# The gate vector's turn as a full product in the PSUM pair of the second turn, and K's first pieces reordered with shorter fillers

## The chip, the cores and the metric

The kernel runs on one core of one Trainium2 chip. The time is the device time of one execution in microseconds (us).

Names used below: PE is the matmul engine, PEld its weight load, ACT, DVE and POOL are ScalarE, VectorE and GpSimd, SP is the engine whose queue (SPq) issues most DMAs. "Landing" is the time at which the last of a DMA's semaphore increments stands in the trace. Times within an execution are counted from the start of the profiled span.

## The reference, cut to what matters

```
g = sigmoid((x * gate_w).sum(-1, keepdims=True))
a = linear_attention(x, wqkv, wo)     # q, k, v = x @ wqkv; phi(k), phi(q); ...
b = mixer_mlp(x, w1, w2, w3, w4)
return g * a + (1 - g) * b            # x: 1 x 2048 x 640, bf16
```

The first work of the kernel is K, the product of x with the K columns of `wqkv`, for 16 chunks of 128 rows each. The gate's logit is one more column of that product: `gate_w`, turned into a column, is put into column 640 of K's weights.

## The kernel before

PE needs x transposed. The first chunk is turned on PE (five 128x128 transposes); the other 15 come through transposing DMAs. `gate_w` arrives as 5 rows of 128 and is turned on PE into 128x5. Fillers (`warmup`: products of ones into a PSUM pair that nobody reads) keep PE busy while data arrives; they are meant to make its clock rise early.

```
    load_x(0, 1)                                   # SP queue
    aq.dma_start(g5[:], ...)                       # ACT queue: gate_w, 5 x 128
    load_wk(sp, 1); load_wk(aq, 0); load_wk(aq, 2); load_wk(sp, 3); load_wk(aq, 4)
    for c0, c1 in ((1, 2), (2, 3), (3, 4), (4, 6), (6, 8), (8, 12), (12, 16)):
        load_xT(c0, c1)                            # transposing DMAs on SP's queue
    ...
    warmup(6)                                      # six 512-wide fillers
    warmup(3, P)                                   # three 128-wide
    kp = pair()
    turns = [(pair()[:, 0, :].bitcast(BF16), a, b) for a, b in ((0, 2), (2, DC))]
    tg = warm[:, 0, :].bitcast(BF16)               # the fillers' own pair
    for n, (ptb, a, b) in enumerate(turns):
        for dc in range(a, b):
            nc.tensor.transpose(ptb[...], x_sb[:, 0, dc * P:(dc + 1) * P], ident[:])
        nc.vector.tensor_copy(xT[:, a:b, 0:P], ...)
        if n == 0:
            nc.tensor.transpose(tg[:, 0:DC], g5[:], ident[0:DC, 0:DC])
            nc.vector.tensor_copy(wk_sb[:, :, D], tg[:, 0:DC])
    warmup(3, P)
    for dc in range(DC):
        k_mm(kp, 0, (dc,))                         # one piece: two products, 320 and 321 wide
        if dc < DC - 1:
            warmup(1, 2 * P)
    k_evac(kp, 0)
    for c in range(1, NCH):                        # chunks 1 to 15, no fillers
        pt = pair()
        k_mm(pt, c, range(DC))
        k_evac(pt, c)
```

Of the kernel before, what the change touches and what calls it, by code (L numbers as in the profile page):

```python
# [9 lines left out]
BF16 = mybir.dt.bfloat16  # L10
# [6 lines left out]
def kernel(  # L17
# [13 lines left out]
    nc = tc.nc  # L31
    P = 128
    S, D = A_x.shape[1], A_x.shape[2]
# [6 lines left out]
    DC = D // P  # L40
    HD = D // 2
# [19 lines left out]
    const = ctx.enter_context(tc.tile_pool(name="const", bufs=1))  # L61
# [7 lines left out]
    def pair():  # L69
        return ps.tile([P, 2, 512], F32, name="pp")  # L70
# [14 lines left out]
    r_bf = const.tile([P, TS], BF16)  # L85
    ident = const.tile([P, P], BF16)
    g5 = const.tile([DC, P], BF16)
    mhalf = const.tile([P, CPT], F32)
    hmask = const.tile([P, H], F32)
    zbd = const.tile([P, DC, H], BF16)  # L90
# [16 lines left out]
    wk_sb = st1.tile([P, DC, D + 16], BF16)  # L107
# [73 lines left out]
    def phi(dst, src, n):  # L181
        e = e_p.tile([P, 1024], BF16, name="e")
        ev = e[:, 0:n]
        if len(src.shape) == 3:
            ev = ev.rearrange("p (h e) -> p h e", h=src.shape[1])
        nc.scalar.activation(ev, src, ACT.Exp)  # L186
        nc.vector.tensor_scalar(e[:, 0:n], e[:, 0:n], 1.0, 1e-6, op0=ALU.min, op1=ALU.add)
        nc.vector.scalar_tensor_tensor(dst, src, 0.0, ev, op0=ALU.max, op1=ALU.add)  # L188

    def k_mm(pt, c, dcs, hfs=(0, 1), last=DC - 1):  # L190
        for dc in dcs:
            for hf in hfs:
                n = HD + hf
                nc.tensor.matmul(pt[:, hf, 0:n], lhsT=xT[:, dc, c * P:(c + 1) * P],  # L194
                                 rhs=wk_sb[:, dc, hf * HD:hf * HD + n], start=(dc == 0), stop=(dc == last))

    def k_evac(pt, c):
        nc.scalar.copy(ylog[:, c:c + 1], pt[:, 1, HD:HD + 1])
        phi(pk[:, c, :].rearrange("p (h e) -> p h e", h=2), pt[:, :, 0:HD], D)

    warm = pair()
    one = nc.const_aps.tensor(1.0, (P, TS), BF16)

    def warmup(n, w=TS):
        for i in range(n):
            nc.tensor.matmul(warm[:, 1, 0:w], lhsT=one[:, 0:P], rhs=one[:, 0:w], start=True, stop=True)  # L206

    warmup(6)
    warmup(3, P)
    kp = pair()  # L210
    turns = [(pair()[:, 0, :].bitcast(BF16), a, b) for a, b in ((0, 2), (2, DC))]
    tg = warm[:, 0, :].bitcast(BF16)
    for n, (ptb, a, b) in enumerate(turns):
        for dc in range(a, b):
            nc.tensor.transpose(ptb[:, (dc - a) * P:(dc - a + 1) * P], x_sb[:, 0, dc * P:(dc + 1) * P], ident[:])
        nc.vector.tensor_copy(xT[:, a:b, 0:P], ptb[:, 0:(b - a) * P].rearrange("p (c s) -> p c s", c=b - a))
        if n == 0:
            nc.tensor.transpose(tg[:, 0:DC], g5[:], ident[0:DC, 0:DC])
            nc.vector.tensor_copy(wk_sb[:, :, D], tg[:, 0:DC])
    warmup(3, P)  # L220
    for dc in range(DC):
        k_mm(kp, 0, (dc,))
        if dc < DC - 1:
            warmup(1, 2 * P)
    k_evac(kp, 0)
    for c in range(1, NCH):
        pt = pair()
        k_mm(pt, c, range(DC))
        k_evac(pt, c)
# [375 lines left out]
```

## Time and profile before

| | before |
|---|---|
| median of 3 runs | 265.8 us (265.54 to 266.0) |
| span of the profiled execution | 264.0 us |
| PE busy | 99% of the span |
| chain of waits that ended last | 97% PE |
| start of K chunk 0, of chunk 1, of chunk 8 | 4.82, 7.12, 16.66 us |

The first lines are the page's busy times and its chain by engine (shares of the span), of the kernel before.

```profile
PE 260.3 (99%) x1744; PEld 161.8 (61%) x1744; DVE 139.5 (53%) x271; ACT 85.1 (32%) x126; POOL 21.9 (8%) x67
...
PE 97%; ACT 1%; DVE 0%; issue 0%
```

PE sets the time from front to end. Busy PE is not useful PE, though: the fillers count as busy too. The next lines are the timeline of PE at the front (start us, duration us, engine, source line, operation, shapes, count). Durations include each product's pipeline, so the rate is read from one start to the next.

```profile
0.83 3.04 PE L206 MATMUL pp<-const-bfloat16-1.0 128*128 128x512 bf16 x9 [0.83 <-PEq L589]
3.66 0.42 PE L215 MATMUL pp<-ident,x_sb 128*128 128x128 bf16 x2
4.01 0.18 PE L218 MATMUL pp<-ident,g 5*128 5x5 bf16 x1
4.13 0.50 PE L215 MATMUL pp<-ident,x_sb 128*128 128x128 bf16 x3
4.55 0.48 PE L206 MATMUL pp<-const-bfloat16-1.0 128*128 128x128 bf16 x3
4.82 0.74 PE L194 MATMUL pp<-wk_sb,xT 128*128 128x320 bf16 x2
5.36 0.42 PE L206 MATMUL pp<-const-bfloat16-1.0 128*128 128x256 bf16 x1
5.57 0.57 PE L194 MATMUL pp<-wk_sb,xT 128*128 128x320 bf16 x2
5.97 0.27 PE L206 MATMUL pp<-const-bfloat16-1.0 128*128 128x256 bf16 x1
6.08 0.44 PE L194 MATMUL pp<-wk_sb,xT 128*128 128x320 bf16 x2
6.36 0.27 PE L206 MATMUL pp<-const-bfloat16-1.0 128*128 128x256 bf16 x1
6.46 0.44 PE L194 MATMUL pp<-wk_sb,xT 128*128 128x320 bf16 x2
6.74 0.27 PE L206 MATMUL pp<-const-bfloat16-1.0 128*128 128x256 bf16 x1
6.85 0.57 PE L194 MATMUL pp<-wk_sb,xT 128*128 128x320 bf16 x3
```

(The window ends at 7.2 us; the third product of the last line is the first of chunk 1, at 7.12.) Two things are to be seen. First, a piece of K and its filler take 0.75 us from 4.82 to 5.57, and 0.38 us from 6.08 to 6.46, where the next piece starts: the clock doubles in between. The packed trace's clock record begins at 5.83 us, at full speed, and that is called the rise. The mean clock that the page and each run list leaves the time before it out: it reads 1.0 here in spite of the slow start. Second, the 5-row gate turn (the 5*128 line) leaves holes: the transpose before it starts at 3.77 and the next after it at 4.13, for one product that has five columns; and the 128-wide filler behind the last transpose (4.32) starts only at 4.55, since it writes the PSUM pair that DVE must first empty (its copy ended at 4.50).

### The profile page before, as it was taken

What the parts mean: (1) busy time and instruction counts of PE and PEld (TensorE: products, weight loads), DVE (VectorE), ACT (ScalarE), POOL (GpSimd) and SP (SyncE); (2) the same over time, 40 slices, a digit from 0 to 9 for tenths busy, and PEclk for the clock granted to TensorE, in tenths of its full rate; (3) what the DMA queues carried; (4) which work ended last, traced back from release to release, by engine and by line L of the source; (5) the groups of instructions that cost most, each with busy time, mean ns of one, the idle gap of its engine ahead of it and who ended that gap; (6) DMA issues with size and microseconds to landing.
All of it is one profiled execution on the core that took longest, in us unless ns stands there. A gap on an engine that the chain in (4) does not pass through costs nothing.

```text
span 264.0 us, 4272 instructions
## 1 busy us (share of the span) xinstructions
PE 260.3 (99%) x1744; PEld 161.8 (61%) x1744; DVE 139.5 (53%) x271; ACT 85.1 (32%) x126; POOL 21.9 (8%) x67
## 2 busy tenths in 40 slices
PE   8999999999999999999999999999999999999995
PEld 4777555788754654556667555667565576555743
DVE  1688778899948597964503455413356223112132
ACT  1555554321165725612502221412131332142100
POOL 7100120012210040001000001000001000000000
PEclk9999999999999999999999999999999999999999
DMA  7999987016673726700132000051100051100011
GB/s 200 179 208 370 375 252 298 0 29 123 124 101 75 79 51 161 239 0 2 25 75 77 25 0 2 0 99 52 50 0 2 0 101 52 50 0 2 0 50 50
DMA packets 46285, 23.62 MB, mean 89 GB/s; under 512 B 35770, under 2 KB 45626, under 8 KB 46266
## 3 DMA queue, kind: packets, MB, share of 16 engines
q1 hardware_dynamic: 45824, 22.86, 34.1%
q10 hardware_dynamic: 442, 0.49, 0.5%
q8 instruction: 13, 0.21, 0.4%
q14 instruction: 6, 0.05, 0.1%
HBM read 12.21 MB, written 2.62 MB: 56 GB/s over the span
## 4 chain that ended last, share of the span: by engine, by line
PE 97%; ACT 1%; DVE 0%; issue 0%
PE pp L484 21%; PE pp L464 21%; PE pp L194 8%; PE pp L311 8%; PE pp L417 8%; PE pp L448 8%; PE pp L345 8%; PE pp L236 8%; PE pp L206 2%; PE pp L472 1%; PE pp L493 1%; ACT m_sb L385 1%; PE pp L364 1%; PE pp L251 0%; DVE oc L512 0%; PE pp L383 0%
## 5 line engine op out<-in xcount | busy, mean ns | idle before, releaser
L464 PE MATMUL pp<-lnxT,w_sb 128*128 128x512 bf16 x260 | 60.4, 379 | 0.0
L484 PE MATMUL pp<-w_sb,h 128*128 128x256 bf16 (+3 forms) x416 | 58.0, 299 | 0.1
L466 ACT ACTIVATE h<-pp 128x1024 bf16<-128x1024 f32 (+1 forms) x28 | 26.9, 962 | 82.2 <-PE pp L464 82.2
L484 PEld LDWEIGHTS <-h 128*128 128x128 bf16 x416 | 39.3, 98 | 18.0 <-issue 1.3
L464 PEld LDWEIGHTS <-w_sb 128*128 128x128 bf16 x260 | 25.5, 98 | 26.8
L500 DVE SCALAR_TENSOR_TENSOR oc<-pp,omg,x 128x640 bf16<-128x640 f32 x14 | 12.0, 881 | 41.4 <-ACT h2x L475 21.3
L451 DVE SCALAR_TENSOR_TENSOR x<-pp,gate,x 128x640 f32<-128x640 f32 x16 | 13.9, 868 | 29.4 <-PE pp L448 29.4
L420 DVE TENSOR_TENSOR x<-pp,x_sb 128x640 f32<-128x640 f32 x16 | 13.1, 820 | 22.6 <-PE pp L417 22.6
L186 ACT ACTIVATE e<-pp 128x640 bf16<-128x640 f32 (+1 forms) x26 | 21.5, 827 | 9.6 <-PE pp L236 9.6
L448 PE MATMUL pp<-m_sb,pqT 128*128 128x320 bf16 x160 | 24.3, 299 | 0.0
L417 PE MATMUL pp<-w_sb,hsT 128*128 128x320 bf16 x160 | 23.9, 299 | 0.1
L194 PE MATMUL pp<-wk_sb,xT 128*128 128x320 bf16 (+1 forms) x160 | 22.9, 302 | 0.0
L311 PE MATMUL pp<-x_sb,pk 128*128 128x320 bf16 (+1 forms) x160 | 22.3, 300 | 0.0
L236 PE MATMUL pp<-xT,hsT 128*128 128x512 bf16 x100 | 21.7, 379 | 0.0
L311 PEld LDWEIGHTS <-pk 128*128 128x128 bf16 x160 | 18.8, 117 | 3.5
L417 PEld LDWEIGHTS <-hsT 128*128 128x128 bf16 x160 | 15.6, 98 | 8.2 <-issue 0.2
L448 PEld LDWEIGHTS <-pqT 128*128 128x128 bf16 x160 | 15.7, 98 | 7.7
L194 PEld LDWEIGHTS <-xT 128*128 128x128 bf16 x160 | 15.8, 99 | 6.1
L345 PE MATMUL pp<-lnxT,w_sb 128*128 128x512 bf16 x80 | 17.9, 379 | 0.0
L236 PEld LDWEIGHTS <-hsT 128*128 128x128 bf16 x100 | 11.8, 118 | 9.7
L281 POOL TENSOR_SCALAR rstd<-mv 128x4 f32<-128x4 f32 (+1 forms) x11 | 3.4, 314 | 156.5 <-DVE mv L287 156.5
L188 DVE SCALAR_TENSOR_TENSOR pk<-pp,e 128x640 bf16<-128x640 f32 x16 | 13.2, 825 | 1.7
(77 smaller groups left out, 194.9 us busy)
## 6 DMA issues: line engine op xcount, KB each, us to landing
out_dram<-oc SPq DMA_DIRECT2D x14, 160.0 KB, 1.8
w_sb<-in_B_w_dram SPq DMA_DIRECT2D x1, 2080.0 KB, 10.0
w_sb<-in_B_w_dram SPq DMA_DIRECT2D x1, 1296.0 KB, 8.4
x_sb<-in_A_x_dram SPq DMA_DIRECT2D x2, 640.0 KB, 10.4
x_sb<-in_A_x_dram SPq DMA_DIRECT2D x1, 1120.0 KB, 7.9
wo_sb<-in_A_wo_dram SPq DMA_DIRECT2D x6, 160.0 KB, 6.0
w_sb<-in_B_w_dram SPq DMA_DIRECT2D x1, 864.0 KB, 5.7
hsT<-in_A_wqkv_dram SPq DMA_DIRECT2D x1, 800.0 KB, 5.3
```

Of the source, the lines that this page charges most:

```text
L186: nc.scalar.activation(ev, src, ACT.Exp)
L188: nc.vector.scalar_tensor_tensor(dst, src, 0.0, ev, op0=ALU.max, op1=ALU.add)
L194: nc.tensor.matmul(pt[:, hf, 0:n], lhsT=xT[:, dc, c * P:(c + 1) * P], rhs=wk_sb[:, dc, hf * HD:hf * HD + n], start=(dc == 0), stop=(dc == ...
L236: nc.tensor.matmul(pt[:, t % 2, :], lhsT=wq_sb[:, dc, :].rearrange("p (m j) -> p j m", j=DC)[:, j], rhs=xT[:, dc, t * TS:(t + 1) * TS], st ...
L311: nc.tensor.matmul(pt[:, hf, 0:HD + hf], lhsT=w, rhs=x_sb[:, c, hf * HD:(hf + 1) * HD + hf], start=(c == 0), stop=(c == NCH - 1))
L345: nc.tensor.matmul(pt[:, i, :], lhsT=w, rhs=lnxT[t][:, dc, :], start=(dc == 0), stop=(dc == DC - 1))
L417: nc.tensor.matmul(pt[:, hf, 0:HD], lhsT=hsT[:, fc, 2 + c * P:2 + (c + 1) * P], rhs=w2_sb[:, fc, hf * HD:(hf + 1) * HD], start=(fc == 0), ...
L448: nc.tensor.matmul(pt[:, hf, 0:HD], lhsT=pqT[:, j, c * P:(c + 1) * P], rhs=m_sb[:, j, hf * HD:(hf + 1) * HD], start=(j == 0), stop=(j == D ...
L451: nc.vector.scalar_tensor_tensor(x1, pt[:, :, 0:HD], gate[:, c:c + 1], x1, op0=ALU.mult, op1=ALU.add)
L464: nc.tensor.matmul(pt[:, k, :], lhsT=w3_sb[:, dc, fc * P:(fc + 1) * P], rhs=lnT[:, dc, :], start=(dc == 0), stop=(dc == DC - 1))
L466: nc.scalar.activation(h2[:, 2 * i * TS:(2 * i + n) * TS], pt[:].rearrange("p h e -> p (h e)")[:, 0:n * TS], ACT.Gelu_apprx_tanh)
L484: nc.tensor.matmul(dst, lhsT=st[t]["h2"][:, fc * TS + cc * P:fc * TS + (cc + 1) * P], rhs=w4_sb[:, fc, a:b], start=start and fc == 0, stop ...
```

## The change

The intent: close both holes (a full 128-row product in the pair of the second turn instead of a 5-row one in the fillers' pair), start earlier with fewer fillers, and take K's pieces in the order in which their weights land.

```diff
+    g5z = const.tile([P, P], BF16)
...
+    nc.vector.memset(g5z[:], 0.0)
+    nc.vector.tensor_copy(g5z[0:DC, :], g5[:])
-    warmup(6)
+    warmup(5)
     warmup(3, P)
...
-        if n == 0:
-            nc.tensor.transpose(tg[:, 0:DC], g5[:], ident[0:DC, 0:DC])
-            nc.vector.tensor_copy(wk_sb[:, :, D], tg[:, 0:DC])
+        if b == DC:
+            nc.tensor.matmul(pt[:, 1, 0:DC], lhsT=g5z[:], rhs=ident[:, 0:DC], start=True, stop=True)
...                                                # after the copy of the second turn:
+        if b == DC:
+            nc.vector.tensor_copy(wk_sb[:, :, D], pt[:, 1, 0:DC])
-    warmup(3, P)
-    for dc in range(DC):
-        k_mm(kp, 0, (dc,))
-        if dc < DC - 1:
-            warmup(1, 2 * P)
+    warmup(4, P)
+    for n, dc in enumerate((1, 0, 3, 2, 4)):
+        if n > 1:
+            warmup(1, P)
+        k_mm(kp, 0, (dc,), first=1, last=4)
+    warmup(2, P)
```

(`k_mm` now takes the first piece as an argument; the order stands inline here.)

More of the change, by code (lines that the diff above doesn't have):

```diff
@@ L188, in phi, with k_mm @@
         nc.vector.scalar_tensor_tensor(dst, src, 0.0, ev, op0=ALU.max, op1=ALU.add)
-    def k_mm(pt, c, dcs, hfs=(0, 1), last=DC - 1):
+    def k_mm(pt, c, dcs, first=0, last=DC - 1):
         for dc in dcs:
-            for hf in hfs:
+            for hf in range(2):
                 n = HD + hf
                 nc.tensor.matmul(pt[:, hf, 0:n], lhsT=xT[:, dc, c * P:(c + 1) * P],
-                                 rhs=wk_sb[:, dc, hf * HD:hf * HD + n], start=(dc == 0), stop=(dc == last))
+                                 rhs=wk_sb[:, dc, hf * HD:hf * HD + n], start=(dc == first), stop=(dc == last))
     def k_evac(pt, c):
@@ L199, in k_evac @@
         phi(pk[:, c, :].rearrange("p (h e) -> p h e", h=2), pt[:, :, 0:HD], D)
+    k0_order = (1, 0, 3, 2, 4)
     warm = pair()
@@ L206, in warmup @@
             nc.tensor.matmul(warm[:, 1, 0:w], lhsT=one[:, 0:P], rhs=one[:, 0:w], start=True, stop=True)
-    warmup(6)
+    nc.vector.memset(g5z[:], 0.0)
+    nc.vector.tensor_copy(g5z[0:DC, :], g5[:])
+    warmup(5)
     warmup(3, P)
     kp = pair()
-    turns = [(pair()[:, 0, :].bitcast(BF16), a, b) for a, b in ((0, 2), (2, DC))]
-    tg = warm[:, 0, :].bitcast(BF16)
-    for n, (ptb, a, b) in enumerate(turns):
+    turns = [(pair(), a, b) for a, b in ((0, 2), (2, DC))]
+    for pt, a, b in turns:
+        ptb = pt[:, 0, :].bitcast(BF16)
         for dc in range(a, b):
             nc.tensor.transpose(ptb[:, (dc - a) * P:(dc - a + 1) * P], x_sb[:, 0, dc * P:(dc + 1) * P], ident[:])
+        if b == DC:
+            nc.tensor.matmul(pt[:, 1, 0:DC], lhsT=g5z[:], rhs=ident[:, 0:DC], start=True, stop=True)
         nc.vector.tensor_copy(xT[:, a:b, 0:P], ptb[:, 0:(b - a) * P].rearrange("p (c s) -> p c s", c=b - a))
-        if n == 0:
-            nc.tensor.transpose(tg[:, 0:DC], g5[:], ident[0:DC, 0:DC])
-            nc.vector.tensor_copy(wk_sb[:, :, D], tg[:, 0:DC])
-    warmup(3, P)
-    for dc in range(DC):
-        k_mm(kp, 0, (dc,))
-        if dc < DC - 1:
-            warmup(1, 2 * P)
+        if b == DC:
+            nc.vector.tensor_copy(wk_sb[:, :, D], pt[:, 1, 0:DC])
+    warmup(4, P)
+    for n, dc in enumerate(k0_order):
+        if n > 1:
+            warmup(1, P)
+        k_mm(kp, 0, (dc,), first=k0_order[0], last=k0_order[-1])
+    warmup(2, P)
     k_evac(kp, 0)
```

## The prediction

> **What bounds the kernel now.** PE: 99% of a 264.0 us span on the page, 97% of the chain of waits. The listing of waits for PE gives only the start (0.8 us). So a shift at the front reaches the end unless something else steps in. The change touches only the first 7 us, before the second K chunk.
>
> **The front, from PE's timeline, start to start.** At first a 512-wide filler takes 0.427 us, a 128-wide one 0.107, a 320-wide K product 0.267. From 5.84 us on they take half (0.136 and, 256 wide, 0.109). This is the clock gate of the Trainium skill, "TensorE: Matmul & The Clock Gate", Part 1; its two rates agree with this trace. Transposes start at 3.67, the first K piece at 4.83, the second K chunk at 7.12. Two holes are the gate vector's: about 0.14 us around its 5-row turn (3.77 to 4.21), and 0.13 us where the filler waits for VectorE to empty the PSUM pair that turn shared with the fillers (4.32 to 4.61).
>
> **What the change does.**
> - One 512-wide filler less: transposes start 0.43 us earlier (3.24), just after the x chunk lands (3.09).
> - Gate turn as a full 128-row product in another pair: both holes go, about 0.27 us. Its memset and copy run on an idle VectorE before 3 us.
> - Fillers before K: four 128-wide for three, +0.11 us. PE is ready at about 4.30, but the first weight piece lands at 4.50 (piece 1, now first; piece 0, before first, at 4.76). K starts at about 4.55, 0.28 us earlier; PE idles 0.25 us instead.
> - Fillers between the pieces: 0.54 us become three 128-wide plus two behind, about 0.33 us. Part of that is lost if the clock still rises at 5.84. The second chunk then starts at about 6.83 instead of 7.12: 0.3 us gained. Its x landed at 6.60, so nothing holds it.
>
> **How much reaches the end.** Little. The K chunks read x through transposing DMAs, whose issue does not depend on PE. The one for chunks 8 to 11 is issued at 9.41 and takes 7.0 us to land: 16.44. Before, PE loads chunk 8's first weights at 16.53, only 0.09 us later. Moved 0.3 us forward, PE would want them at 16.23 and must wait; its product can start at about 16.60 instead of 16.66. All other landings have at least 0.38 us of slack. So of 0.3 us at 7 us I expect 0.06 us behind chunk 8, the rest as a new wait of PE there. The landing can jitter, so up to 0.3 us may survive in some runs.
>
> **Prediction: 265.7 us, range 265.3 to 266.2.** Faster by over 2%: 0.01; within 2%: 0.98; slower by over 2%: 0.01.
>
> **What the profile would show.**
> - Transposes from 3.24 us, no hole at the gate turn.
> - PE idle about 0.25 us ahead of K's first product, until the weights' DMA; K at 4.55.
> - Second chunk at 6.8 to 6.9.
> - A PE wait on the transposing DMA at chunk 8 near 16.5 us, and all starts behind it within 0.1 us of before. If chunk 8 starts at 16.37, the DMA landed earlier and the gain is 0.3 us.
>
> **What would make it wrong.** The clock gate: if the hole before K, or the 5-wide product's low activity, makes the clock rise later, each K product until then costs 0.13 us more; a whole window of 3.4 us (that page's figure) at half rate would lose up to 1.7 us (estimate). If it rises earlier, 0.2 us more are gained at the front and lost again at chunk 8. A late x chunk (0.05 to 0.15 us of margin) would move everything.

## The result

The changed kernel took 265.97 us (median of 4 runs, 265.76 to 266.23), the kernel before 265.7 us in its 4 runs. The ratio is 1.0009, 95% interval 0.9992 to 1.0027: the same. A ratio is the mean time of one kernel's runs over that of the other's of the same rounds, so it is not quite the ratio of the medians quoted. With the two repeats below the changed kernel has 16 runs of mean 265.93 us.

First the chain by engine on the page of the changed kernel, to be read against the 97% PE of before.

```profile
PE 91%; SPq 3%; DMA 3%; ACT 1%; DVE 0%; issue 0%
```

Then its PE timeline at the front.

```profile
0.83 2.61 PE L208 MATMUL pp<-const-bfloat16-1.0 128*128 128x512 bf16 x8 [0.83 <-PEq L595]
3.24 0.74 PE L219 MATMUL pp<-ident,x_sb 128*128 128x128 bf16 x5
3.77 0.21 PE L221 MATMUL pp<-ident,g5z 128*128 128x5 bf16 x1
3.84 0.59 PE L208 MATMUL pp<-const-bfloat16-1.0 128*128 128x128 bf16 x4
4.22 0.89 PE L195 MATMUL pp<-wk_sb,xT 128*128 128x320 bf16 x4
4.95 0.22 PE L208 MATMUL pp<-const-bfloat16-1.0 128*128 128x128 bf16 x1
5.56 0.43 PE L195 MATMUL pp<-wk_sb,xT 128*128 128x320 bf16 x2 [0.40 <-DMA wk_sb<-in_A_wqkv_dram]
...
6.49 0.28 PE L208 MATMUL pp<-const-bfloat16-1.0 128*128 128x128 bf16 x2
6.75 2.49 PE L195 MATMUL pp<-wk_sb,xT 128*128 128x320 bf16 x17
```

The front did what it was meant to do: transposes from 3.24, a gate product that costs 0.07 us to the next start, K at 4.22, chunk 1 at 6.75 instead of 7.12, 0.37 us earlier. PE now waits for weights inside the first chunk (0.40 us before piece 3).

Then the changed kernel's chain of waits from 9 to 40 us (start us, us, what), and its PE timeline around chunk 8.

```profile
8.14 1.71 SPq L122
9.85 0.04 issue
9.89 7.03 DMA xT<-in_A_x_dram
16.92 0.05 issue
16.97 11.07 PE pp L195 x80
```

```profile
14.78 1.80 PE L195 MATMUL pp<-wk_sb,xT 128*128 128x320 bf16 x12
16.97 2.22 PE L195 MATMUL pp<-wk_sb,xT 128*128 128x320 bf16 x15 [0.39 <-DMA xT<-in_A_x_dram]
```

The chain now runs over the transposing DMA of chunks 8 to 11. It was issued at 9.89 and landed at 16.92, and chunk 8 started at 16.97, where the kernel before had started it at 16.66 without a wait (its landing: 16.43). The kernel before shows one run of products there:

```profile
14.75 4.52 PE L194 MATMUL pp<-wk_sb,xT 128*128 128x320 bf16 x32
```

So at chunk 1 PE was 0.37 us ahead of the kernel before, and at chunk 8 it was 0.31 us behind it: 0.68 us were lost between the two. Of these 0.11 went at chunk 4, whose x landed at 10.91, and 0.55 at chunk 8. From there on both executions run alike: the last product of the kernel starts 244.44 us after chunk 8 in the one, 244.45 in the other.

That one trace leaves a question. Was the DMA late because of the change, or by scatter, and would the front's gain show if chunk 8 did not hold it?

### The profile page after: what moved, and what is told of

It reads as the page before. It is cut to its first block, busy times and chain, and to the rows that moved or that the text cites. A ratio compares the mean times of both kernels' runs of the same rounds, so it can differ in the third digit from the quotient of the medians.

```text
span 264.3 us, 4277 instructions
## 1 busy us (share of the span) xinstructions
PE 259.8 (98%) x1745; PEld 161.4 (61%) x1745; DVE 139.8 (53%) x273; ACT 85.1 (32%) x126; POOL 21.8 (8%) x67
## 4 chain that ended last, share of the span: by engine, by line
PE 91%; SPq 3%; DMA 3%; ACT 1%; DVE 0%; issue 0%
PE pp L490 21%; PE pp L470 21%; PE pp L317 8%; PE pp L423 8%; PE pp L454 8%; PE pp L351 8%; PE pp L242 8%; PE pp L195 4%; SPq L122 3%; DMA xT<-in_A_x_dram 3%; PE pp L478 1%; PE pp L499 1%; ACT m_sb L391 1%; PE pp L370 1%; PE pp L257 0%; DVE oc L518 0%
## 5 line engine op out<-in xcount | busy, mean ns | idle before, releaser
L188 DVE TENSOR_SCALAR e<-e 128x640 bf16<-128x640 bf16 (+1 forms) x26 | 9.5, 365 | 9.4 <-ACT e L187 8.1
```

## The experiments

Theory 1: PE is held at chunk 8 by a landing that does not depend on PE; the front's gain is given back there. Theory 2: the change itself makes the DMA chain late. Theory 3: its lateness is scatter between executions. A further rival: the front's gain in the trace was the luck of an early clock rise (4.33 us here, 5.83 before), not the change's.

The twelve runs came in three sets of four: a1, b1, c1, d1 on one chip; then a2, c2, e1, e2, and last b2, c3, g1, o1, both on another chip. The first set shares 11 executions of the kernel before, of mean 265.88 us. The other two share 12 (those of the second set and one more), of mean 266.18 us.

### a1, a2: the changed kernel again

No edit.

> The changed kernel once more, to see what of its one trace repeats. Theory 1 (PE is held at K chunk 8 by the transposing DMA of chunks 8 to 11, so the front's gain is given back there): chunk 8 starts within 0.1 us of that landing, 16.4 to 17.0 us, and the ratio to before is 0.999 to 1.002. Theory 2 (the change itself slows the SyncE queue's DMA chain by 0.4 us): that chain is late again, the second transposing DMA is again issued in 1.78 us, and landing is again 16.9. Theory 3 (the chain's lateness is scatter between executions): issue times of 1.3 to 1.5 us and landing near 16.4, chunk 8 at about 16.5.

> The changed kernel once more, for its scatter (265.3 to 266.6 us so far, wider than before's 265.5 to 266.2) and one more clock rise. The traces so far give the rise of the clock at 3.8 to 6.7 us, another in each execution; with the durations of the traces I estimate that chunk 1 starts at 6.64 for every rise before 5.4 us (held by the landing of its x), and at 6.8 to 7.5 for a rise of 5.8 to 7.2. Theory P (the clock's phase makes the scatter): the trace's chunk 1 start fits that within 0.1 us. Theory M (the changed front at times misses a window of the clock): a rise later than 7.3 us shows up. Ratio 0.999 to 1.002 in either case.

a1: 265.9 us median, ratio 1.0002 (0.9986 to 1.0018). Chunk 8's x landed at 16.27, chunk 8 started at 16.32: held, as theory 1 says, though just below its 16.4 to 17.0. The second transposing DMA took 1.26 us to issue, not 1.78, which speaks for theory 3. a2: 265.8 us, ratio 0.9987 (0.9969 to 1.0004); landing 17.26, start 17.30. The clock rose at 4.21 and 4.98, so theory M had no sign. Chunk 1 started at 6.66 and 7.17, in each case 0.05 us after its own x landed (6.61 and 7.13). Theory P's estimate assumed a landing of 6.60 and missed a2 by 0.53 us: late landings did that (of weight piece 3 at 5.67, then of the x), not the clock. The chain of a2 from 7.96 us:

```profile
7.96 1.64 SPq L122
9.60 0.04 issue
9.65 7.61 DMA xT<-in_A_x_dram
17.26 0.05 issue
17.30 11.07 PE pp L195 x80
```

### e1, e2: the kernel before again

No edit; one profiled execution each.

> The kernel before, for its clock rise and its front. Estimate from the traces' durations: chunk 1 at 6.64 (held by its x) for a rise before 4.9 us, 6.9 for 5.4, 7.1 for 5.8, 7.5 for 6.7, 7.8 for 7.2. Theory P: the trace fits within 0.1 us. A rival, that the kernel before always starts chunk 1 after 7.1, falls if the rise is early and chunk 1 starts at 6.7.

> The same once more, another clock rise; the same line of estimates holds.

e1 took 266.38 us: clock rise 6.80, chunk 1 at 7.60, landing for chunk 8 17.25, chunk 8 at 17.29 (0.16 us late). e2 took 265.9 us: rise 6.16, chunk 1 at 7.28, landing 16.69, chunk 8 at 16.82, not held. The unchanged kernel lands as late as 17.25. Theory 2 has no support: in three traces of the kernel before the landing was 16.43, 16.69 and 17.25, in three of the changed one 16.27, 16.92 and 17.26. Both chunk 1 starts fit the estimates within 0.1 us. No early rise was caught with the old front, so that rival was not tested.

### b1, c1, then c2, b2, c3: chunk 8's x cut loose

The same edit in both kernels (b: before, c: changed):

```diff
-    for c0, c1 in ((1, 2), (2, 3), (3, 4), (4, 6), (6, 8), (8, 12), (12, 16)):
+    for c0, c1 in ((1, 2), (2, 3), (3, 4), (4, 6), (6, 8), (8, 10), (10, 12), (12, 16)):
```

> The kernel before, with the transposing DMA of chunks 8 to 11 cut into two of two chunks. Theory 1: chunk 8's x lands near 14 us instead of 16.44, and PE of the kernel before was held there only when the DMA was late, so 0 to 0.2 us are gained: ratio 0.9992 to 1.000. A rival that the cut itself makes DMA better or worse overall would show as more than 0.3 us either way.

> The changed kernel with the same cut. Theory 1: nothing holds PE at chunk 8, so the 0.3 to 0.4 us of the front reach the end: 265.2 to 265.5 us, ratio 0.9982 to 0.9990, and 0.2 to 0.5 us less than the kernel before with the same cut. Rival: the front's gain in the one trace was the clock's luck, or was never there; then the time equals that of the kernel before with the cut within 0.1 us.

> The changed kernel with chunk 8's x cut loose, once more. If late landings at chunk 8 make the changed kernel's slow executions (266.2 to 266.6), this one has none above 266.1, and its mean is 0.1 to 0.2 us under the changed kernel's of the same rounds. If not, its scatter is the same.

> The kernel before with chunk 8's x cut loose, once more, beside the changed kernel with the same cut. Theory 1, mended by the traces (the landing for chunk 8 scatters from 16.3 to 17.3 us in both kernels and caps either): the cut takes from the kernel before only its late landings, 0.05 to 0.2 us: ratio 0.999 to 1.000. Chunk 8 starts 9.54 us after chunk 1 with no wait; chunk 1 at 7.1 to 7.8 if the clock rises after 5.8, at about 6.7 if it rises before 5.

> The changed kernel with the cut. Theory 1: under the kernel before with the cut by 0.1 to 0.4 us in the same rounds, ratio to before 0.998 to 0.999, and no execution above 266.1. Rival (batch 2's 0.9977 came from slow rounds of before): no difference from the kernel before with the cut.

| run | set | ratio to before | mean us | clock rise | chunk 1 | chunk 8's x landed | chunk 8 |
|---|---|---|---|---|---|---|---|
| b1 (before, cut) | 1 | 0.9998 (0.9985 to 1.0011) | 265.88 | 6.73 | 7.56 | 13.95 | 17.10 |
| c1 (changed, cut) | 1 | 0.9998 (0.9986 to 1.0010) | 265.80 | 6.01 | 6.81 | 14.05 | 16.35 |
| c2 (changed, cut) | 2 | 0.9977 (0.9962 to 0.9992) | 265.57 | 3.86 | 6.86 | 14.51 | 16.41 |
| b2 (before, cut) | 3 | 0.9981 (0.9965 to 0.9997) | 265.71 | 5.45 | 7.08 | 13.85 | 16.61 |
| c3 (changed, cut) | 3 | 0.9980 (0.9963 to 0.9996) | 265.65 | 4.94 | 7.47 | 14.15 | 17.02 |

In all five the x of chunk 8 lands about 1.9 us or more before it is wanted, and chunk 8 follows chunk 1 by 9.53 to 9.55 us without a wait. The PE timeline of c1 around chunk 8 shows one run of products where the changed kernel had a gap.

```profile
14.71 2.48 PE L195 MATMUL pp<-wk_sb,xT 128*128 128x320 bf16 x17
```

Three results follow. The cut helps where the landing was late: uncut, chunk 8's x landed at 16.54 us on average in the four traces up to the first set, and at 17.12 in the five of the second and third; with the kernel before (b) the cut gained nothing in the first set and 0.5 us in the third (0.19%; by the interval 0.1 to 0.9 us), where 0.05 to 0.2 had been expected. With the changed kernel c2 had no execution above 265.84 and lay 0.35 us under a2 (265.92; the difference has a standard error of 0.17), where 0.1 to 0.2 had been expected; c1 lay 0.10 under a1. The cut also costs something: the time from the start of the kernel's last product to the end of the span is 3.03 to 3.04 us in all five traces with it and 2.91 to 2.93 in all nine without, 0.1 us lost at the very end. Why is not shown. Secondly, the whole change on top of the cut is worth 0.08 us in the first set and 0.06 us in the third (b minus c), where 0.2 to 0.5 and 0.1 to 0.4 us had been expected; pooled, 17 runs of c against 11 of b (c2 has no b in its own set), it is 0.12 us with a standard error of 0.09, which is not told from nothing. Theory 1 is right about where the changed kernel waits, and wrong that taking the wait away would lay bare the front's 0.3 to 0.4 us. Thirdly, c3 shows one reason. Its own PE timeline:

```profile
4.55 0.88 PE L195 MATMUL pp<-wk_sb,xT 128*128 128x320 bf16 x4
5.27 0.22 PE L208 MATMUL pp<-const-bfloat16-1.0 128*128 128x128 bf16 x1
6.27 0.43 PE L195 MATMUL pp<-wk_sb,xT 128*128 128x320 bf16 x2 [0.78 <-DMA wk_sb<-in_A_wqkv_dram]
```

Piece 3 of the weights landed at 6.23 and the x of chunk 1 at 7.42, and chunk 1 started at 7.47: the quick front stood waiting for its data. In c2 too chunk 1 waited for its x (landed at 6.82, start 6.86), in c1 it did not. That the same holds in the executions that were not traced is not shown. c3 also had one execution at 266.19, against the expectation of none above 266.1.

### d1: more filler behind chunk 0

```diff
     warmup(2, P)
+    warmup(2)                                     # 0.43 us at the full clock
     k_evac(kp, 0)
```

> The changed kernel with two more 512-wide fillers (0.43 us at the full clock) behind chunk 0. Theory 1: they are absorbed in the wait at chunk 8, time within 0.15 us of the changed kernel's, chunk 8 again at its landing. Rival (all front work counts in full): 0.43 us more, ratio to before about 1.0025.

266.13 us median, mean 266.14, ratio 1.0011 (0.9998 to 1.0024); a1 in the same rounds had a mean of 265.90. In its trace chunk 1 started at 7.00, the landing for chunk 8 was 16.54 and chunk 8 started at 16.59, 0.05 us behind it as theory 1 says. The mean rose by 0.24 us of the 0.43 put in, between the two expectations, and the interval reaches towards both: partly absorbed, and not decisive alone.

### g1: the gate's turn alone

```diff
+    g5z = const.tile([P, P], BF16)                # and its memset and copy, as in the change
-            nc.tensor.transpose(tg[:, 0:DC], g5[:], ident[0:DC, 0:DC])   # with its copy
+            nc.tensor.matmul(pt[:, 1, 0:DC], lhsT=g5z[:], rhs=ident[:, 0:DC], start=True, stop=True)
```

Fillers and order are those of the kernel before.

> The kernel before with the gate vector's turn alone changed. Both holes of 3.77 to 4.61 us are gone and PE is ready for K at about 4.6 instead of 4.83. K's first product is then held by the landing of weight piece 0 (4.4 to 4.8 in the traces) and its second half by the gate column's copy (about 5.0), so at most 0.2 us are gained at chunk 1 with a late clock rise and none with an early one; behind chunk 8 under 0.1 us: ratio 0.9985 to 1.001. Rival (the 0.27 us of holes count in full): chunk 1 0.27 us earlier at the same clock rise (at a rise of 5.8: 6.85 instead of 7.12).

The PE timeline of g1:

```profile
3.67 0.74 PE L218 MATMUL pp<-ident,x_sb 128*128 128x128 bf16 x5
4.20 0.21 PE L220 MATMUL pp<-ident,g5z 128*128 128x5 bf16 x1
4.27 0.48 PE L207 MATMUL pp<-const-bfloat16-1.0 128*128 128x128 bf16 x3
4.68 0.65 PE L195 MATMUL pp<-wk_sb,xT 128*128 128x320 bf16 x2
```

The holes are gone: transposes and gate product run through from 3.67 to 4.27, where before the fillers behind the turns began only at 4.55. But K starts at 4.68, 0.14 us earlier and not 0.27, because piece 0 of the weights landed at 4.64, and the second product of that piece starts 0.285 us after the first instead of 0.267, waiting for the gate column's copy. Chunk 1 started at 6.69 (rise at 5.13), where the durations of the old front put it at about 6.77 for such a rise (an estimate from the same traces). Chunk 4 was held for 0.08 us (landing 10.82) and chunk 8 for 0.66 by a landing at 16.94. The ratio, 0.9983 (0.9966 to 1.0001), lies just under the range expected and does not part it from before.

### o1: the changed kernel with the old order of pieces

```diff
-    k0_order = (1, 0, 3, 2, 4)
+    k0_order = (0, 1, 2, 3, 4)
```

> The changed kernel with K's first pieces in the old order 0, 1, 2, 3, 4. K's first product then waits for piece 0, 0.2 to 0.4 us later than piece 1: K starts at 4.5 to 4.8, not at 4.22 to 4.54, but the gate column's copy (about 4.5) holds the second half in either order, so 0.0 to 0.25 us are lost at chunk 1 with a late clock rise, and none with an early one, where the landing of chunk 1's x (6.6 to 7.1) holds. Ratio within 0.001 of the changed kernel's.

Ratio 1.0002 (0.9984 to 1.0019), a2's was 0.9987 against nearly the same runs of before. That is 0.0015 apart where 0.001 had been expected, with intervals that overlap: no difference is shown. K started at 4.46, 0.04 us after piece 0 landed; chunk 1 at 6.79. The listing of waits for PE shows what the front waits for now:

```profile
PE pp L195 <- DMA xT<-in_A_x_dram: 0.9, 1, 0.9
PE pp L208 <- PEq L595: 0.8, 1, 0.8
PE pp L195 <- DMA wk_sb<-in_A_wqkv_dram: 0.7, 2, 0.5
```

(The columns are total us, times, longest.) Chunk 8's x landed at 17.49, the latest of all, and this is the slowest profiled execution, 266.6 us.

### What all the traces say together

The last product starts 244.43 to 244.45 us after chunk 8 in all 14 traces. For the nine without the cut, the time of the profiled execution is the start of chunk 8 plus 249.07 to 249.09 us (with the cut it is 249.17 to 249.31). The six of the two kernels themselves:

| trace | clock rise | chunk 1 | chunk 8's x landed | chunk 8 | time |
|---|---|---|---|---|---|
| before | 5.83 | 7.12 | 16.43 | 16.66 | 265.74 |
| e2 (before) | 6.16 | 7.28 | 16.69 | 16.82 | 265.9 |
| e1 (before) | 6.80 | 7.60 | 17.25 | 17.29 | 266.38 |
| a1 (changed) | 4.21 | 6.66 | 16.27 | 16.32 | 265.39 |
| changed | 4.33 | 6.75 | 16.92 | 16.97 | 266.06 |
| a2 (changed) | 4.98 | 7.17 | 17.26 | 17.30 | 266.39 |

In these nine everything up to chunk 8 decides the time, and everything behind it is constant to 0.02 us. In the traces, what moves chunk 8 is when the clock rises and when x and the weights land (in b2 K started only at 5.15, 0.04 us after weight piece 0). The executions of one kernel scatter by 1.3 us; that the same things make all of that is argued, since most were not traced. A version that beats both kernels clearly was not found; the cut, in either, was 0.2% quicker in the second and third set and equal in the first.

## Why the prediction was right or wrong

The range held the time (265.97 in 265.3 to 266.2), and "within 2%" held. Point by point:

- **The front.** "Transposes from 3.24 us, no hole at the gate turn": so it was in all traces of the changed kernel (3.23 or 3.24), and the 0.3 us forecast at chunk 1 was 0.37 in the first trace (6.75 for 7.12). The size is no proof of the forecast: in that trace the clock rose at 4.33, not 5.83, and by the estimate given for e1 the old front would have reached chunk 1 at about 6.64 with such a rise (at about 6.8 with the weight landings of that trace; both are estimates). The match is luck, unless the change itself brings the rise forward (below).
- **The wait at chunk 8.** "A PE wait on the transposing DMA at chunk 8 near 16.5 us" was right in kind and in all three traces of the changed kernel.
- **The size of what survives** failed. The step "its product can start at about 16.60 instead of 16.66" took one trace's landing (16.44 there, 16.43 read again) for a fixed number and let jitter only help ("up to 0.3 us may survive"). The landing lay anywhere from 16.27 to 17.49 us in nine executions, so "all starts behind it within 0.1 us of before" was off by 0.31 us the other way. "All other landings have at least 0.38 us of slack" failed with it: chunk 4 too was held, by 0.08 to 0.12 us, in three traces (changed, g1, o1; landings 10.82 to 10.95, before: 10.39).
- **"PE idles 0.25 us instead", "K at 4.55".** In the first trace piece 1 landed at 4.03, not 4.50, and K started at 4.22; then the second product of the piece waited for DVE's copy of the gate column and started at 4.54. In a2, c1 and c2 that product also started at 4.54, 0.05 us after the copy ended (4.49). (The listing of waits of a1 puts 0.2 us down to DVE, but there piece 1 landed at 4.50, after the copy's end, and K's first product, which does not read the column, started 0.04 us later: that wait was for the weights.) This wait was created by the change, which puts the gate's turn last; the prediction had not counted it.
- **"Its x landed at 6.60, so nothing holds it."** Wrong in most traces: in five of the six traces of the changed kernel and of its version with the cut (c1 is the exception), chunk 1 started 0.05 us after its x landed, at 6.66 to 7.47.
- **The clock.** "If it rises earlier, 0.2 us more are gained at the front and lost again at chunk 8" is what the first trace shows in kind (rise at 4.33): the clock gained time that the landings took back. At nearly the same rise, c1 (6.01) had chunk 1 at 6.81 and e2 (6.16) at 7.28; the 0.15 us between the rises explain about 0.08 us of those 0.47 (an estimate: work at half rate loses half the time). Against the first trace of the kernel before, whose clock rose even earlier than c1's (5.83), c1 is 0.31 us ahead, as forecast. So in these pairs the new front is quicker by itself when the clock rises late; c1 is the only trace of it with a late rise.

What stays open: with the old front the clock rose at 5.45 to 6.80 us (five traces), with the new one at 3.77 to 6.01 (eight, with d1 and o1); g1, the old front with the new turn, had 5.13. In only 2 of the 40 pairs of an old and a new trace is the old one's rise the earlier. If the thirteen rises were dealt to the two fronts at random, 4 of the 1287 ways would give so few, so chance alone is unlikely; but no experiment was made for it, and whether and how the change does it no run settles. The kernel before has unprofiled runs at 265.44 us, which by the constant above mean a chunk 8 at about 16.4 and so an early rise there too; that is argued, not traced. Also open is why chunk 8's x landed 0.6 us later in the second and third set: they ran on another chip than the first, and later.

## What to carry to other kernels

When a bound engine is sped up at the front, list for every later stage when its data lands and when it is wanted: the smallest margin (0.09 us here, nine microseconds behind the edit) caps the gain, and a landing read from one trace is a draw and not a constant, so take it from several executions. Look at cutting the first transfers that the faster engine will run into before shaving the engine's own work (here worth 0.2% in two of three sets), and read the end of the trace too, where the cut cost 0.1 us. Compare fronts at the same clock rise, or a lucky phase passes for a gain; and ask whether the change moves the rise.

## What the Trainium skill lacked or had wrong

- "TensorE: Matmul & The Clock Gate", Part 1, says the clock rises around 4 us into sustained activity, give or take 500 ns. Its two rates agree (0.267 us for a 320-wide product, then 0.136), but in 14 traces of this family the rise came 2.9 to 6.0 us after PE's first product (3.77 to 6.80 on the span's clock, first product at 0.83): a spread of plus or minus 1.5 us. The same section's free-running window (3.4 us; the rises spread over 3.0) fits that better than its own 500 ns.
- The same page, Part 2 ("LDWEIGHTS"), says that a load of 32 rows takes as long as one of 128. The load of 5 rows took 0.098 us here, and the 128-row loads around it, which overlap products, 0.10 to 0.15; but next to full products the 5-row turn cost 0.24 us from the start before it to its own, and 0.11 us to the next, where the 128-row product cost 0.11 and 0.07. No page has a figure for going from full to few rows and back ("TensorEngine Tiling (Array Packing)" only names a drain when the tiling mode changes; no run here shows that this is it). That the row count alone causes it was not tried apart: the turn also changed from a transpose to a product.
- "DMA: Bandwidth & Descriptors", section "DMA Transpose (X-bar)", gives no scatter. The same transposing DMA of four chunks landed 6.9 to 7.9 us after its issue, at 16.27 to 17.49 us, in nine executions.
